# A retention and channel-mix kernel: the pieces behind the head in another order, block 3's values scaled on VectorE

## The chip, the core and the metric

The kernel runs on one core of a Trainium2 chip. The metric is the device time of one execution in microseconds (us); lower is better. Before the change the runs gave 153.27, 153.72 and 153.78 us, median 153.72.

## What is computed

There are 4 sequences of 768 tokens and 8 heads of 64 channels. The first half is a recurrence over tokens in which a 64x64 state of each head decays by its own factor; the second half is a channel mix on 512 channels with 1024 hidden ones.

```
state = gamma * state + outer(k[t], v[t])          # per sequence and head
x[t]  = scale * q[t] @ state                       # heads side by side: 512 channels
xk = mu_k * x + (1 - mu_k) * x_prev                # x_prev: the token before
xr = mu_r * x + (1 - mu_r) * x_prev
out = sigmoid(xr @ w_r) * (relu(xk @ w_k)**2 @ w_v)
```

## The kernel before

**Tiling.** The tokens are cut into 12 blocks of 256, three for each sequence; block n belongs to sequence n // 3. A block is computed in closed form: masked scores within it, and a state carried from the block before. The channel mix then runs on the block's output, which is kept transposed (channels in partitions, tokens along the line) in float32.

**An order written by hand.** The program is a list of short words, the string ORDER (lines 24 to 81). Line 755 goes through the words and calls one small function for each, so the order of the words is the order of instructions on every engine. A word is a code, its block and further indices, then `~v`, `~a`, `~p` or `~s` for the engine (VectorE, ScalarE, GpSimd, SyncE) and `@` with the numbers of the PSUM banks that a product writes. The framework adds the semaphores: each instruction waits for what it reads, and for readers of what it overwrites. Engines otherwise run freely, each through its own list.

The words that matter, with n the block:
- `lk`, `lq`, `lv` load keys, queries and values (line 222; keys and queries are cast to float16 on the way, so they go by GpSimd's queue); `wk`, `wr`, `wv` load the weights of the mix. The buffers are rings of 4, so `lq.11` waits until `Tq.7` has read block 7's queries.
- `vs` scales the values by powers of gamma (line 253), into a ring of 3.
- `Tq`, `Tk` transpose queries and keys on TensorE; `Eq`, `Ek` copy them out of PSUM on ScalarE (line 241).
- `S` makes scores (lines 318, 331), `M` masks them on VectorE (lines 347, 354). `C` makes the state's products from keys and scaled values (lines 366, 384), `U` adds them to the carried state (line 419), `G` decays it for the next block (line 424 on ScalarE, line 428 on VectorE).
- `I`, `Y`, `J` make the block's output: from the carried state, from the masked scores, and from the state again (lines 441, 462, 478). `D` scales it into xT (lines 507, 514), `dx` takes differences of neighbouring tokens (line 529), `X.n.0` and `X.n.1` mix four slices each for xk and xr (line 558); for block 0 `t` and another form of `X` do it (lines 542, 552).
- `K` are the first channel products (lines 572, 582), `Qa` takes the relu out of PSUM and `Qb` squares it, both on ScalarE (lines 591, 599, 603). `R` is the gate's product (line 612), `s` its sigmoid on ScalarE (line 618). `V` are the value products (line 624), `O` multiplies value and gate on VectorE (line 630), `st` stores (line 637). `Vc`, `Oc`, `sc` are V, O, st on half the columns, for the last piece.
- `z` are products of zeros on TensorE in the head.

Blocks 3 and 4, 6 and 7, and 9 and 10 are mixed as pairs: one product of 512 columns instead of two of 256. TensorE's pieces have two kinds of form: K, R, V and Vc use the array whole (128x128), T, S, C, I, Y and J use halves or quarters of it (128x64, 64x128, 64x64), several at a time.

Any two pieces in one PSUM bank follow one another: the second starts when ScalarE or VectorE has read out the first. There are eight banks.

The first 82 words are the head; K.0.0, the first channel product, follows just behind.

Of the kernel before, what the change touches and what calls it, by code (L numbers as in the profile page):

```python
# [43 lines left out]
O.1.0~v Tq.6@23 Eq.6~a Tk.6@01 Ek.6~a st.0.0~s lk.7~p st.1.0~s V.1.1.0@5 V.1.1.1 O.1.1~v s.2.0~a
R.2.1@2 s.2.1~a lv.5~p X.3.0.0~v X.3.0.3~v Tk.7@67 Ek.7~a G.4~a S.6@01 M.6~v Tk.5@45 Ek.5~a vs.5~v
V.2.0.0@2 K.3.2@3 Qa.3.2~a K.3.0@6 S.5.0@45 M.5.0~v S.5.1@01 C.5@3 U.5.0~v K.3.3@7 Qb.3.2~a Qa.3.0~a
lq.7~p K.3.7@6 Qa.3.3~a Qa.3.7~a lv.6~p lq.8~p vs.6~v M.5.1~v V.2.0.1 st.0.1~s I.5@67 O.2.0~v
st.2.0~s C.6@45 U.6.0~a U.6.1~v U.6.2~v K.3.6@3 Qa.3.6~a lk.9~p X.3.1.3~v Y.5 Tq.7@01 Eq.7~a U.6.3~v
# [1 line left out]
Qb.3.7~a Qa.3.1~a Qb.3.1~a dx.5~v K.3.4@0 K.3.5@1 Qa.3.5~a X.5.0.0~v X.5.0.3~v R.3.1@4 s.3.1~a  # L50
lv.7~p Qa.3.4~a X.5.0.1~v Qb.3.4~a R.3.0@1 R.4.0@4 s.3.0~a s.4.0~a Qb.3.0~a X.5.0.2~v vs.7~v K.5.2@0
S.7@67 st.1.1~s M.7~v Qb.3.5~a Y.6 Qb.3.6~a lv.10~p C.7@45 U.7.0~v X.5.1.1~v Qa.5.2~a K.5.0@1
R.4.1@6 Qa.5.0~a D.6~v s.4.1~a V.4.0.0@0 V.4.0.1 V.3.1.0@1 U.7.1~v Qb.5.0~a X.5.1.3~v U.7.2~v I.7@23
X.5.1.2~v U.7.3~v Tq.8@67 Eq.8~a X.5.1.0~v O.4.0~v lv.8~p vs.8~v Qb.5.2~a lq.10~p lk.8~p Tk.8@45
Ek.8~a V.3.1.1 V.3.0.0@0 C.8@67 O.3.1~v st.2.1~s st.3.1~s Y.7 dx.6~v D.7~v Tq.10@45 V.3.0.1 Eq.10~a
G.7~a dx.7~v X.6.0.2~v V.4.1.0@1 R.5.1@4 s.5.1~a K.5.3@2 Qa.5.3~a R.5.0@4 U.8.0~v O.3.0~v V.4.1.1
lv.9~p lk.10~p lq.9~p Tk.10@23 s.5.0~a U.8.1~v X.6.0.1~v Ek.10~a X.6.0.0~v Tk.9@45 Ek.9~a K.5.1@7
Qa.5.1~a X.6.0.3~v K.6.0@0 lq.11~p Qb.5.1~a Qa.6.0~a U.8.2~v I.8@23 vs.9~v S.8@45 M.8~v O.4.1~v
st.4.1~s K.6.4@7 Qa.6.4~a vs.10~v X.6.1.2~v K.6.2@6 C.9@45 Qa.6.2~a Qb.6.2~a U.9.0~a Y.8 U.9.1~v
D.8~v U.9.2~v U.9.3~v X.6.1.3~v Qb.5.3~a Tq.9@01 V.5.1.0@6 V.5.1.1 O.5.1~v Eq.9~a lk.11~p K.6.3@7  # L60
Qa.6.3~a K.6.7@0 Qa.6.7~a V.5.0.0@7 C.10@01 Qb.6.0~a X.6.1.0~v S.9@45 M.9~v G.9~a Qb.6.3~a Tq.11@23
Eq.11~a V.5.0.1 dx.8~v X.6.1.1~v st.4.0~s K.6.1@6 Qb.6.7~a Qa.6.1~a Qb.6.1~a X.8.0.3~v X.8.0.0~v
U.10.0~v U.10.1~v K.6.5@2 Qa.6.5~a st.3.0~s lv.11~s K.6.6@6 Qa.6.6~a Qb.6.6~a R.6.0@3 s.6.0~a
O.5.0~v U.10.2~v U.10.3~v R.7.0@6 s.7.0~a R.6.1@7 s.6.1~a I.9@01 X.8.0.2~v S.10@23 Tk.11@45 Ek.11~a
X.8.0.1~v K.8.1@7 Qb.6.5~a Qa.8.1~a Qb.8.1~a vs.11~v st.5.1~s K.8.0@6 C.11@45 M.10~v Qb.6.4~a
X.8.1.0~v X.8.1.2~v Y.9 D.9~v G.10~a U.11.0~v st.5.0~s U.11.1~v U.11.2~v Qa.8.0~a I.10@23 V.6.1.0@7
V.6.1.1 O.6.1~v V.6.0.0@0 V.6.0.1 I.11@45 S.11@67 M.11~v dx.9~v V.7.1.0@1 V.7.1.1 Y.10 D.10~v
dx.10~v X.9.0.3~v X.9.0.0~v Y.11 Qb.8.0~a X.9.0.2~v R.7.1@6 s.7.1~a X.9.0.1~v V.7.0.0@7 V.7.0.1
K.8.3@6 O.7.0~v X.9.1.0~v D.11~v X.8.1.1~v Qa.8.3~a Qb.8.3~a K.8.2@2 Qa.8.2~a Qb.8.2~a X.8.1.3~v
dx.11~v X.11.1.0~v X.11.1.1~v X.9.1.1~v V.8.1.0@6 K.9.2@3 X.11.0.0~v K.9.6@7 Qa.9.6~a V.8.1.1  # L70
Qa.9.2~a Qb.9.2~a X.11.0.3~v K.9.5@7 K.9.3@3 K.9.0@2 Qa.9.0~a Qb.9.6~a V.8.0.0@4 V.8.0.1 Qb.9.0~a
Qa.9.5~a Qb.9.5~a Qa.9.3~a O.7.1~v st.7.1~s X.9.1.2~v X.11.0.1~v O.6.0~v K.9.7@5 R.8.1@7 s.8.1~a
# [727 lines left out]
```

## Time and profile before

| | before |
|---|---|
| median of the runs | 153.72 us |
| the profiled execution, its own time | 153.78 us |
| its span, first to last instruction | 152.0 us |
| start of K.0.0 | 18.99 us |
| end of TensorE's last product | 148.85 us |
| TensorE, VectorE, ScalarE, GpSimd busy | 144.9, 127.9, 103.8, 55.3 us |
| granted clock of TensorE | 1.00 |

The span leaves out 1.78 us of the execution's own time around it. Engines work at the same time, so their busy times don't add up. A matmul's end is modelled, and one may look busy while it waits for its operands; how far products stand apart tells more than how long each lasts. The chain that ended last is followed from the last instruction back to what released it, and each row gives a start, a length and the line.

### The profile page before, as it was taken

What the parts mean: (1) busy time and instruction counts of PE and PEld (TensorE: products, weight loads), DVE (VectorE), ACT (ScalarE), POOL (GpSimd) and SP (SyncE); (2) the same over time, 40 slices, a digit from 0 to 9 for tenths busy, and PEclk for the clock granted to TensorE, in tenths of its full rate; (3) what the DMA queues carried; (4) which work ended last, traced back from release to release, by engine and by line L of the source; (5) the groups of instructions that cost most, each with busy time, mean ns of one, the idle gap of its engine ahead of it and who ended that gap; (6) DMA issues with size and microseconds to landing.
All of it is one profiled execution on the core that took longest, in us unless ns stands there. A gap on an engine that the chain in (4) does not pass through costs nothing.

```text
span 152.0 us, 5541 instructions
## 1 busy us (share of the span) xinstructions
PE 144.9 (95%) x2426; PEld 83.2 (55%) x2426; DVE 127.9 (84%) x212; ACT 103.8 (68%) x195; POOL 55.3 (36%) x65
## 2 busy tenths in 40 slices
...
GB/s 134 220 229 196 208 227 195 169 245 211 197 166 206 222 261 113 240 314 201 231 173 125 4 46 278 101 45 35 0 4 0 4 0 202 212 0 0 147 134 138
DMA packets 45624, 22.16 MB, mean 146 GB/s; under 512 B 37400, under 2 KB 41248, under 8 KB 45600
## 3 DMA queue, kind: packets, MB, share of 16 engines
...
q8 instruction: 19, 0.31, 0.9%
...
## 4 chain that ended last, share of the span: by engine, by line
PE 73%; DMA 12%; POOL 11%; issue 1%; DVE 0%; POOLq 0%
PE ps L624 27%; PE ps L572 14%; DMA v<-in_v_dram 12%; PE ps L612 12%; PE ps L582 8%; PE ps L278 3%; POOL q L235 3%; POOL k L230 2%; PE ps L441 2%; POOL vs L253 2%; POOL v L230 2%; PE ps L366 1%; PE ps L462 1%; PE ps L642 1%; PE ps L318 1%
## 5 line engine op out<-in xcount | busy, mean ns | idle before, releaser
L624 PE MATMUL ps<-wv,k2s 128*128 128x512 f16 x184 | 44.1, 380 | 0.0
L591 ACT ACTIVATE kr<-ps 128x512 f32<-128x512 f32 x48 | 27.9, 594 | 13.0 <-PE ps L582 7.1
L624 PEld LDWEIGHTS <-k2s 128*128 128x128 f16 x184 | 17.1, 98 | 18.9 <-ACT k2s L603 0.4
L630 DVE SCALAR_TENSOR_TENSOR os<-ps,rs 128x512 f32<-128x512 f32 x23 | 15.6, 684 | 11.9 <-ACT rs L618 9.4
L612 PE MATMUL ps<-wr,xr 128*128 128x512 f16 x96 | 23.5, 379 | 0.0
L572 PE MATMUL ps<-xk,wk 128*128 128x512 f16 x96 | 23.3, 379 | 0.0
L582 PE MATMUL ps<-xk,wk 128*128 128x256 f16 x192 | 23.2, 273 | 0.0
L618 ACT ACTIVATE rs<-ps 128x512 f32<-128x512 f32 x24 | 13.7, 597 | 13.0 <-PE ps L612 12.4
L230 POOL DMA_DIRECT2D k<-in_k_dram x20 | 17.8, 902 | 10.9 <-PE ps L384 6.8
L582 PEld LDWEIGHTS <-wk 128*128 128x128 f16 x192 | 18.1, 98 | 3.7
L558 DVE SCALAR_TENSOR_TENSOR xr<-dx,mu,xT 128x256 f16<-128x256 f32 (+1 forms) x32 | 17.9, 577 | 0.1
L241 ACT COPY qT<-ps 128x1024 f16<-128x1024 f16 (+1 forms) x13 | 12.3, 946 | 8.2 <-PE ps L278 7.8
L230 POOL DMA_DIRECT2D v<-in_v_dram x18 | 16.0, 912 | 3.7 <-DVE a L354 1.9
L558 DVE SCALAR_TENSOR_TENSOR xk<-dx,mu,xT 128x256 f16<-128x256 f32 (+1 forms) x32 | 17.0, 579 | 0.2
L572 PEld LDWEIGHTS <-wk 128*128 128x128 f16 x96 | 9.1, 98 | 10.8 <-issue 0.5
L603 ACT ACTIVATE k2s<-kr 128x512 f16<-128x512 f32 x24 | 14.8, 631 | 0.3
L612 PEld LDWEIGHTS <-xr 128*128 128x128 f16 x96 | 9.0, 98 | 10.7 <-issue 0.5
L354 DVE TENSOR_TENSOR a<-ps,c_sb 128x1024 f16<-128x1024 f32 (+1 forms) x14 | 14.6, 1065 | 0.2 <-PE ps L331 0.2
L599 ACT ACTIVATE k2s<-kr 128x512 f16<-128x512 f32 x24 | 14.5, 627 | 0.3
L241 ACT COPY kT<-ps 128x1024 f16<-128x1024 f16 (+1 forms) x13 | 12.2, 946 | 2.8 <-PE ps L272 2.0
L529 DVE TENSOR_TENSOR dx<-xT 128x1024 f32<-128x1024 f32 x11 | 13.4, 1222 | 0.2
L253 DVE TENSOR_TENSOR vs<-v,csm_sb 128x1024 f16<-128x1024 f32 x10 | 12.2, 1216 | 0.4 <-DMA v<-in_v_dram 0.4
...
## 6 DMA issues: line engine op xcount, KB each, us to landing
out_dram<-os SPq DMA_DIRECT2D x23, 256.0 KB, 2.5
v<-in_v_dram POOLq DMA_DIRECT2D x18, 256.0 KB, 7.7
q<-in_q_dram POOLq DMA_DIRECT2D x11, 256.0 KB, 8.1
...
```

The source lines that it names most:

```text
L230: e.dma_start(out=dst[:, :, i * D : i * D + D], in_=src[:, i * P : i * P + P].rearrange("h p d -> p h d"),)
L241: e.copy(out=out, in_=in_)
L253: e.tensor_tensor(out=VS(n), in0=V32(n).rearrange("p h (i d) -> p i h d", i=2), in1=gks[:, int(half(n) or wide(n)), :, :, None].to_broadca ...
L354: nc.vector.tensor_tensor(out=a_full(n)[:, i, :, j0:j1], in0=pairs(banks("S", n, i, j0))[:, :, j0:j1], in1=(below if wide(n) else causal[: ...
L558: nc.vector.scalar_tensor_tensor(out=XM[w](k)[:, j, t0:t1], in0=DX(k)[:, j, t0:t1], scalar=mu[:, w * NCO + j : w * NCO + j + 1], in1=x[:, ...
L572: nc.tensor.matmul(banks("K", n, g), lhsT=wk16[:, co, g * P : g * P + P], rhs=XM[0](k)[:, co, :], start=(co == 0), stop=(co == NCO - 1),)
L582: nc.tensor.matmul(pz[:, i, :], lhsT=wk16[:, co, fo * P : fo * P + P], rhs=XM[0](k)[:, co, m * TM + t0 : m * TM + t1], start=(i == 0 and c ...
L591: nc.scalar.activation(out=kr, in_=banks("K", n, g, *u), func=AF.Relu)
L603: nc.scalar.activation(out=K2(n)[:, w * g : w * g + w, t0:t1], in_=kr.rearrange("p a t -> p (a t)").rearrange("p (i t) -> p i t", i=w), fu ...
L612: nc.tensor.matmul(banks("R", n, tb), lhsT=XM[1](k)[:, co, t : t + P], rhs=wr16[:, co, :], start=(co == 0), stop=(co == NCO - 1),)
L624: nc.tensor.matmul(banks("V", n, tb), lhsT=K2(n)[:, fo, tb * P : tb * P + P], rhs=wv16[:, fo, :], start=(fo == 0), stop=(fo == NFO - 1),)
L630: nc.vector.scalar_tensor_tensor(out=OS(2 * n + tb), in0=banks("V", n, tb), scalar=1.0 / (KSC * KSC), in1=RS(2 * n + tb), op0=ALU.mult, op ...
```

## The change

From K.0.0 on the words stand in another order, and so do the instructions on every engine; many products write other PSUM banks. The head is the same, and the words are the same 638, but for two that go to another engine: `vs.3` runs on VectorE instead of GpSimd, and `G.6` on VectorE instead of ScalarE (one multiplication of 128x256 instead of four scalings of 128x64). No function is changed. The GpSimd queue now issues lk.3, wr, lq.4, lk.4, lv.3, lq.3, lv.4 where it issued lq.4, wr, lk.4, lq.3, lk.3, lv.3, lv.4. The diff, cut to the parts that are spoken of:

```diff
-X.0.0.3~v Ek.2~a K.0.0@2 K.0.1@6 lq.4~p U.1.1~v G.1~a wr~p lk.4~p D.1~v dx.1~v X.1.0.2~v X.1.0.0~v
-K.0.2@3 Qa.0.0~a Qb.0.0~a Qa.0.2~a lq.3~p X.1.0.1~v X.1.0.3~v X.1.1.0~v Qa.0.1~a K.0.3@2 Qa.0.3~a
-lk.3~p vs.2~v Tq.2@3 X.1.1.2~v K.1.3@6 K.1.0@2 C.2@7 U.2.0~v lv.3~p Eq.2~a S.2.1@45 M.2.1~v S.2.0@01
-M.2.0~v Qb.0.3~a lv.4~p K.1.1@3 X.1.1.1~v Qa.1.0~a t.0.1.0~a K.1.2@7 I.2@45 Qb.0.1~a Qa.1.1~a wv.0~p
-Qb.0.2~a Tq.4@23 Eq.4~a Y.2 Qa.1.3~a Qb.1.1~a X.0.1.3~v X.1.1.3~v R.1.1@0 Tk.4@23 Ek.4~a J.2 R.1.0@6
-Qa.1.2~a s.1.0~a X.0.1.2~v X.0.1.1~v X.0.1.0~v R.0.1@1 s.0.1~a s.1.1~a R.0.0@7 s.0.0~a S.4.1@23
-Qb.1.0~a D.2~v dx.2~v X.2.0.2~v X.2.0.0~v S.4.0@45 Tq.3@0 Eq.3~a X.2.0.1~v wv.1~p X.2.0.3~v Tk.3@7
-lq.5~p Ek.3~a K.2.2@1 Qa.2.2~a K.2.3@0 M.4.1~v M.4.0~v Qa.2.3~a Qb.2.3~a lk.6~p S.3.1@67 M.3.1~v
-S.3.0@23 vs.3~p C.3@45 U.3.0~a Qb.2.2~a K.2.1@0 Qa.2.1~a K.2.0@4 Qa.2.0~a I.3@01 lq.6~p vs.4~v
-C.4@67 U.3.1~v X.2.1.1~v V.0.1.0@5 M.3.0~v V.1.0.0@4 G.3~a U.4.0~v I.4@23 X.2.1.3~v U.4.1~v J.3
-Qb.1.3~a Y.4 Qb.2.0~a lk.5~p X.2.1.2~v X.2.1.0~v Y.3 D.3~v dx.3~v V.0.0.0@7 V.0.1.1 O.0.1~v Tq.5@01
-J.4 D.4~v dx.4~v R.2.0@6 Qb.2.1~a V.0.0.1 O.0.0~v X.3.0.1~v Eq.5~a Qb.1.2~a V.1.0.1 X.3.0.2~v
...
-X.3.1.2~v I.6@23 J.5 X.3.1.0~v D.5~v X.3.1.1~v Qb.3.3~a G.6~a V.2.1.0@4 K.3.1@5 V.2.1.1 O.2.1~v
...
-Qa.11.2~a X.11.1.2~v O.8.0~v st.7.0~s st.8.1~s st.8.0~s V.9.1.0@5 V.10.1.0@6 s.10.0~a V.9.1.1
-V.10.0.1 s.9.1~a O.9.1~v st.9.1~s Qb.11.2~a Qb.11.3~a O.10.0~v st.10.0~s R.10.1@0 V.9.0.1 s.10.1~a
-O.9.0~v R.11.1@0 V.10.1.1 Qb.11.1~a V.11.0.0@7 R.11.0@1 s.11.0~a st.9.0~s Vc.11.1.1@5 s.11.1~a
-O.10.1~v st.10.1~s Oc.11.1.1~v V.11.0.1 O.11.0~v st.11.0~s sc.11.1.1~a Vc.11.1.0@0 Oc.11.1.0~v
-sc.11.1.0~s
+X.0.0.3~v Ek.2~a K.0.0@2 Qa.0.0~a U.1.1~v G.1~a D.1~v X.0.1.3~v dx.1~v K.0.2@3 K.0.3@2 Qa.0.3~a
+X.1.0.2~v K.0.1@4 X.1.0.0~v X.1.0.1~v Tq.2@2 Eq.2~a X.1.0.3~v vs.2~v K.1.1@5 S.2.1@67 Qa.0.2~a
+S.2.0@01 Qa.1.1~a Qb.1.1~a C.2@3 K.1.0@2 X.1.1.0~v lk.3~p Tk.3@5 M.2.1~v U.2.0~v I.2@67 wr~p
+Qb.0.0~a M.2.0~v t.0.1.0~a lq.4~p Qa.1.0~a Ek.3~a X.1.1.2~v X.1.1.1~v lk.4~p K.1.3@3 Qa.1.3~a
+Qb.1.3~a X.1.1.3~v Y.2 Qb.0.3~a X.0.1.0~v R.1.1@5 X.0.1.1~v Qa.0.1~a lv.3~p Tq.4@23 Eq.4~a J.2
+X.0.1.2~v R.0.0@0 s.0.0~a R.0.1@4 Tk.4@23 Qb.1.0~a R.1.0@0 lq.3~p Ek.4~a s.0.1~a D.2~v s.1.1~a
+Qb.0.2~a K.1.2@1 Qa.1.2~a dx.2~v X.2.0.3~v S.4.1@23 Qb.0.1~a X.2.0.1~v s.1.0~a S.4.0@67 lv.4~p
+X.2.0.0~v X.2.0.2~v vs.3~v K.2.2@5 K.2.3@4 Tq.3@0 Qa.2.3~a Eq.3~a M.4.0~v M.4.1~v C.3@67 U.3.0~a
+K.2.1@4 vs.4~v Qa.2.2~a S.3.0@01 M.3.0~v U.3.1~v S.3.1@23 M.3.1~v wv.0~p Qa.2.1~a Qb.2.1~a K.2.0@6
+Qa.2.0~a I.3@45 G.3~a C.4@01 X.2.1.2~v V.1.1.0@7 V.1.0.0@6 U.4.0~v I.4@23 U.4.1~v X.2.1.0~v wv.1~p
+lk.6~p X.2.1.1~v J.3 Y.4 X.2.1.3~v Y.3 lk.5~p D.3~v G.4~a dx.3~v V.0.0.0@1 V.0.0.1 Tk.6@45 O.0.0~v
+st.0.0~s J.4 D.4~v Qb.1.2~a lq.6~p V.1.1.1 O.1.1~v dx.4~v V.0.1.0@0 V.0.1.1 V.1.0.1 O.0.1~v Qb.2.2~a
+Qb.2.0~a Ek.6~a V.2.0.0@7 Qb.2.3~a lq.5~p Tq.5@23 Eq.5~a lv.5~p X.3.0.0~v Tk.5@01 st.0.1~s Ek.5~a
+Tq.6@45 Eq.6~a X.3.0.1~v X.3.0.2~v V.2.0.1 R.2.1@2 s.2.1~a X.3.0.3~v K.3.6@0 Qa.3.6~a O.1.0~v vs.5~v
+X.3.1.3~v R.2.0@6 X.3.1.2~v lk.7~p s.2.0~a C.5@0 S.6@23 M.6~v Tk.7@45 U.5.0~v Ek.7~a K.3.0@6 O.2.0~v
+Qa.3.0~a K.3.5@1 Qa.3.5~a X.3.1.0~v X.3.1.1~v K.3.7@6 S.5.1@01 Qa.3.7~a Qb.3.5~a S.5.0@23 lv.6~p
+lq.7~p I.5@45 K.3.2@6 Qb.3.6~a Qa.3.2~a K.3.3@7 M.5.1~v st.1.0~s V.2.1.0@6 V.2.1.1 M.5.0~v Y.5
+vs.6~v lv.7~p st.1.1~s vs.7~v lv.11~s Qa.3.3~a Qb.3.3~a O.2.1~v C.6@23 U.6.0~a U.6.1~v U.6.2~v
+st.2.1~s Tq.7@01 Qb.3.0~a Qb.3.2~a Eq.7~a J.5 D.5~v U.6.3~v dx.5~v X.5.0.3~v st.2.0~s K.3.4@7
+Qa.3.4~a R.4.1@6 s.4.1~a K.3.1@2 G.6~v Qa.3.1~a Qb.3.4~a I.6@45 X.5.0.2~v C.7@01 U.7.0~v R.3.1@3
+Qb.3.1~a s.3.1~a U.7.1~v U.7.2~v R.4.0@2 R.3.0@6 s.3.0~a U.7.3~v X.5.1.2~v V.3.1.0@3 s.4.0~a
+X.5.1.3~v I.7@67 S.7@01 M.7~v lq.11~p V.3.0.0@2 Qb.3.7~a V.3.0.1 lv.9~p lq.10~p X.5.1.0~v X.5.0.1~v
...
+lk.9~p Tk.9@45 Ek.9~a O.4.1~v st.3.1~s V.4.0.0@1 V.4.0.1 R.5.0@2 s.5.0~a O.4.0~v X.6.0.2~v st.4.0~s
+V.5.1.0@3 lq.8~p Tq.8@01 X.6.0.3~v C.8@45 lk.10~p U.8.0~v Eq.8~a C.9@67 K.6.4@2 Qa.6.4~a X.6.1.2~v
...
+vs.11~v vs.10~v I.9@67 S.9@01 M.9~v st.4.1~s Qa.6.7~a V.7.0.0@2 Qb.6.7~a Qb.6.6~a X.8.1.1~v V.7.0.1
+C.10@01 O.7.0~v Eq.11~a G.9~a U.10.0~v U.10.1~v V.6.0.0@4 st.7.0~s V.6.0.1 O.6.0~v U.10.2~v Qa.8.0~a
...
+V.9.0.1 s.9.0~a R.9.1@7 s.9.1~a Qa.11.0~a O.9.1~v st.9.1~s Qb.11.0~a R.11.0@5 Qb.11.3~a Qb.11.1~a
+R.10.1@7 V.10.0.0@1 V.10.0.1 O.9.0~v O.8.1~v K.11.2@0 V.10.1.0@6 s.10.1~a V.10.1.1 st.8.0~s st.9.0~s
+st.8.1~s O.10.1~v O.10.0~v st.10.0~s st.10.1~s V.11.0.0@2 Qa.11.2~a Qb.11.2~a V.11.0.1 s.11.1~a
+s.11.0~a O.11.0~v st.11.0~s Vc.11.1.1@1 Oc.11.1.1~v Vc.11.1.0@6 Oc.11.1.0~v sc.11.1.0~s sc.11.1.1~a
```

More of the change, by code (lines that the diff above doesn't have):

```diff
@@ L43 @@
-J.4 D.4~v dx.4~v R.2.0@6 Qb.2.1~a V.0.0.1 O.0.0~v X.3.0.1~v Eq.5~a Qb.1.2~a V.1.0.1 X.3.0.2~v
[L44 to L48, printed above, removed]
@@ L49 @@
-X.3.1.2~v I.6@23 J.5 X.3.1.0~v D.5~v X.3.1.1~v Qb.3.3~a G.6~a V.2.1.0@4 K.3.1@5 V.2.1.1 O.2.1~v
[L50 to L72, printed above, removed]
@@ L73 @@
-K.9.1@1 R.8.0@7 X.9.1.3~v X.11.0.2~v st.6.1~s O.8.1~v R.9.1@0 R.9.0@6 K.11.0@3 K.11.3@2 s.8.0~a
-Qa.9.1~a Qb.9.1~a Qb.9.3~a V.10.0.0@1 V.9.0.0@7 Qa.11.0~a Qb.11.0~a Qa.11.3~a s.9.0~a K.9.4@6
-R.10.0@2 Qa.9.7~a X.11.1.3~v st.6.0~s K.11.1@5 Qa.11.1~a Qa.9.4~a K.11.2@3 Qb.9.7~a Qb.9.4~a
-Qa.11.2~a X.11.1.2~v O.8.0~v st.7.0~s st.8.1~s st.8.0~s V.9.1.0@5 V.10.1.0@6 s.10.0~a V.9.1.1
-V.10.0.1 s.9.1~a O.9.1~v st.9.1~s Qb.11.2~a Qb.11.3~a O.10.0~v st.10.0~s R.10.1@0 V.9.0.1 s.10.1~a
-O.9.0~v R.11.1@0 V.10.1.1 Qb.11.1~a V.11.0.0@7 R.11.0@1 s.11.0~a st.9.0~s Vc.11.1.1@5 s.11.1~a
@@ new lines @@
+X.5.0.0~v Y.6 Y.7 D.6~v D.7~v dx.6~v K.5.2@0 Qa.5.2~a K.5.0@1 K.5.1@0 Qa.5.0~a Qa.5.1~a lk.8~p
+K.5.3@1 G.7~a Qa.5.3~a dx.7~v V.3.1.1 V.4.1.0@0 lv.8~p O.3.1~v X.5.1.1~v Qb.5.3~a O.3.0~v X.6.0.0~v
+vs.8~v V.4.1.1 R.5.1@1 s.5.1~a Qb.5.1~a Tq.10@23 Eq.10~a vs.9~v X.6.0.1~v Qb.5.0~a Tk.8@67 Ek.8~a
+lk.9~p Tk.9@45 Ek.9~a O.4.1~v st.3.1~s V.4.0.0@1 V.4.0.1 R.5.0@2 s.5.0~a O.4.0~v X.6.0.2~v st.4.0~s
+V.5.1.0@3 lq.8~p Tq.8@01 X.6.0.3~v C.8@45 lk.10~p U.8.0~v Eq.8~a C.9@67 K.6.4@2 Qa.6.4~a X.6.1.2~v
+U.9.0~a U.8.1~v K.6.0@0 Qa.6.0~a K.6.2@2 Qa.6.2~a X.6.1.0~v Qb.6.0~a V.5.0.0@5 K.6.3@2 Qa.6.3~a
@@ new lines @@
+Qb.6.3~a U.9.1~v Qb.5.2~a U.9.2~v U.9.3~v U.8.2~v I.8@67 S.8@01 Qb.6.2~a K.6.1@4 M.8~v X.6.1.1~v
+Qa.6.1~a K.6.6@2 Qa.6.6~a X.6.1.3~v Tk.10@01 Ek.10~a Qb.6.4~a Y.8 Qb.6.1~a D.8~v lq.9~p dx.8~v
+st.3.0~s X.8.0.3~v R.6.1@4 s.6.1~a K.6.5@2 V.5.0.1 Qa.6.5~a Qb.6.5~a X.8.1.3~v V.5.1.1 O.5.1~v
+st.5.1~s R.7.1@4 s.7.1~a lv.10~p S.10@67 X.8.1.2~v Tq.9@23 Eq.9~a lk.11~p Tk.11@01 Ek.11~a X.8.0.2~v
+O.5.0~v st.5.0~s R.6.0@4 X.8.0.0~v s.6.0~a R.7.0@5 s.7.0~a K.6.7@2 M.10~v X.8.0.1~v K.8.0@3 Tq.11@45
+vs.11~v vs.10~v I.9@67 S.9@01 M.9~v st.4.1~s Qa.6.7~a V.7.0.0@2 Qb.6.7~a Qb.6.6~a X.8.1.1~v V.7.0.1
```

9 lines of the change are left out of this document (added).

## Prediction

> **What bounds the kernel now.** I read the page's busy shares first, then the windows for the five stretches behind the head, the waits of TensorE, and the chain that ended last.
>
> ```profile
> span 152.0 us, 5541 instructions
> ...
> PE 144.9 (95%) x2426; PEld 83.2 (55%) x2426; DVE 127.9 (84%) x212; ACT 103.8 (68%) x195; POOL 55.3 (36%) x65
> ```
> ```profile
> 19.00:45.00 26.00, 24.87 (x410) 18.04 (x405) 24.56 (x39) 21.87 (x42) 19.50 (x22) 1.00 1.59 202
> 45.00:67.00 22.00, 22.00 (x411) 11.03 (x409) 21.67 (x29) 15.35 (x29) 14.41 (x17) 1.00 1.35 224
> 67.00:104.00 37.00, 37.00 (x842) 20.73 (x841) 36.27 (x59) 29.62 (x54) 7.14 (x9) 1.00 0.89 136
> 104.00:128.00 24.00, 24.00 (x343) 12.97 (x341) 22.34 (x35) 13.34 (x26) 0.00 (x0) 1.00 0.05 19
> 128.00:152.00 24.00, 20.83 (x120) 11.54 (x118) 7.14 (x13) 11.74 (x22) 0.00 (x0) 1.00 0.31 115
> ```
> ```profile
> PE ps L384 <- DVE vs L253: 0.5, 1, 0.5
> PE ps L478 <- DVE a L354: 0.4, 1, 0.4
> PE ps L384 <- POOL vs L253: 0.3, 1, 0.3
> ```
>
> In a window row the stretch's length is followed by the busy times of TensorE (24.87 in the first), its weight loads, VectorE (24.56), ScalarE and GpSimd, then clock, DMA share and GB/s. The changed part starts with K.0.0 at 18.99 us. From there TensorE idles 26.00 - 24.87 = 1.13 us up to 45 and then never until its last product. VectorE is nearly as full: 24.56 of 26.00, 21.67 of 22.00, 36.27 of 37.00. So TensorE bounds, VectorE stands just behind it, and a new order of the same pieces can win only the 1.13 us, a little that hides inside busy rows, and the tail. The clock column is 1.00 throughout and needs no further thought.
>
> **The tail** keeps its form: two half-width value products (Vc), a scaling each, a store each. Both orders end so, hence 0.
>
> ```profile
> 52.66 0.37 PE ps L278 x32
> 53.04 0.27 PE ps L318 x32
> 53.30 0.29 PE ps L278 x32
> 53.60 0.97 PE ps L624 x4
> 54.56 1.73 PE ps L572 x8
> ...
> 66.85 2.73 PE ps L612 x12
> ...
> 97.26 2.88 PE ps L572 x12
> 100.14 2.59 PE ps L612 x12
> ...
> 121.03 2.59 PE ps L572 x12
> ...
> 127.94 2.71 PE ps L612 x12
> ...
> 148.85 0.02 issue
> 148.87 0.42 DVE os L649
> ```
>
> **Changes of array shape (+0.74 us).** K, R, V and Vc use the whole 128x128 array; the transposes, scores, states and outputs (T, S, C, I, J, Y) use halves or quarters of it. The chain shows what a run of small pieces between whole ones costs beyond its own streaming. Eight whole-array products take 1.73, so four take 0.865; the four just behind small ones take 0.97, 0.10 more. The 32 transposes at 52.66, just behind whole ones, take 0.37; the same form at 53.30, behind other small ones, 0.29, 0.08 less. Together 0.185 for each run. I counted runs in both orders from K.0.0 on: 25 before, 29 after. 4 x 0.185 = 0.74. Bounds: 0, if every added run stands beside a wait that is there anyway, and 0.74.
>
> The Trainium skill, "TensorEngine Tiling (Array Packing)", Key Properties, speaks against this change too: a change of the tiling mode, not merely of the tile, drains TensorE. By that rule the changes from one small shape to another count as well, 65 after and 58 before; at some 0.1 us each that would be +0.7 us. The 0.10 and 0.08 of the chain agree with it.
>
> **Waits that go (-1.68 us).** First the 1.13 us above: C.2 waited for the scaled values of block 2 (0.5), Y.2 for masked scores (0.4), C.3 for GpSimd's scaling of block 3 (0.3). Then waits inside busy rows: twelve whole products stream in 2.59 (100.14, 121.03), but took 2.88, 2.73 and 2.71 in other places, 0.29 + 0.14 + 0.12 = 0.55 us. These are pieces that found their PSUM bank not yet read out. Order decides both kinds, so I strike them and price the new order afresh.
>
> **Waits that come, up to 45 us (+0.89 us).** I went through the new order piece by piece with the durations below.
>
> ```profile
> 18.99 3.67 PE L582 MATMUL ps<-xk,wk 128*128 128x256 f16 x32
> 22.59 0.64 PE L272 MATMUL ps<-c_sb,q 128*64 128x128 f16 x16
> 23.16 1.95 PE L582 MATMUL ps<-xk,wk 128*128 128x256 f16 x16
> 25.59 0.32 PE L384 MATMUL ps<-vs,k 128*64 128x64 f16 x8 [0.48 <-DVE vs L253]
> 25.84 0.62 PE L331 MATMUL ps<-qT,kT 64*128 64x128 f16 x16
> ```
> ```profile
> 20.54 1.23 DVE L529 TENSOR_TENSOR dx<-xT 128x1024 f32<-128x1024 f32 x1
> 21.80 1.68 DVE L558 SCALAR_TENSOR_TENSOR xk<-dx,mu,xT 128x256 f16<-128x256 f32 x4
> 23.39 0.48 DVE L558 SCALAR_TENSOR_TENSOR xr<-dx,mu,xT 128x256 f16<-128x256 f32 x1
> 24.31 1.23 DVE L253 TENSOR_TENSOR vs<-v,csm_sb 128x1024 f16<-128x1024 f32 x1 [0.43 <-DMA v<-in_v_dram]
> ```
>
> - K.1.1, +0.32. TensorE does the four K of block 0 and Tq.2 as before and reaches block 1 at 23.16. VectorE now does X.0.1.3 ahead of dx.1 (about 0.3 more), so the last of the four mixes ends at 23.48 + 0.29 = 23.77. The fourth product of K.1.1 needs it and would start at 23.16 + 0.33 = 23.49; with 0.05 for the release it starts at 23.81.
> - C.2, +0.52. vs.2 cannot start before its values land (24.31 with its wait above; the load is issued in the unchanged head), so C.2 stays at 25.59. Before it the new order puts S.2.1 and S.2.0 (two of the x16 row, 0.55 together) where the old one had K.1.0; K.1.1 leaves at 24.45, the scores have ended at 25.07.
> - I.2, Y.2, R.1.1, R.0.0, K.2.2, Tq.3, S.3.0 and I.4 come out on time by 0.0 to 0.5 us, Tq.3 by 0.05 and S.3.0 by 0.1 behind ScalarE. C.4 waits 0.05 for the masked scores of block 3.
>
> **vs.3 on VectorE, G.6 on VectorE.**
>
> ```profile
> 25.49 10.70 DMA v<-in_v_dram
> 36.19 0.07 issue
> 36.27 1.91 POOL vs L253
> ```
> ```profile
> L253 DVE TENSOR_TENSOR vs<-v,csm_sb 128x1024 f16<-128x1024 f32 x10 | 12.2, 1216 | 0.4 <-DMA v<-in_v_dram 0.4
> L424 ACT ACTIVATE tg<-t,csm_sb 128x64 f16<-128x64 f32 x32 | 8.5, 337 | 0.9 <-DVE t L419 0.9
> L419 DVE TENSOR_TENSOR tg<-ps,tg 128x256 f16<-128x256 f32 x20 | 8.4, 418 | 1.4 <-PE ps L331 0.5 <-PE ps L395 0.5 <-ACT tg L424 0.3
> ```
>
> GpSimd loses 1.9 us and ScalarE four scalings of 337 ns; VectorE gains 1.22 for vs.3 and, by its nearest row (L419), 0.42 for G.6: 1.64 us on an engine that has 1.44 us free up to 45 and 0.33 us between 45 and 67. Behind vs.3 on VectorE stand M.4.0 (frees C.3's bank), M.4.1, vs.4 and M.3.0 (frees C.4's). It is paid from the lead that VectorE has where TensorE does value products (the V pieces need nothing of it), so I book nothing for it alone; where the lead is used up is the next part. One condition: VectorE reaches vs.3 at about 34.95 (from vs.2's end at 25.54: two masks, D.2 and dx.2 at 1.2 each less their overlap, one U, eleven mixes at 0.4), and in this trace the values of block 3 landed at 36.19. In the new order lk.3 and wr go ahead, lv.3 before lq.3. One q load is 256 KB, at the 202 GB/s of the first window 1.3 us, so lv.3 should land near 34.9. This is an estimate, and it just fits.
>
> ```profile
> L230 POOL DMA_DIRECT2D v<-in_v_dram x18 | 16.0, 912 | 3.7 <-DVE a L354 1.9 <-DVE os L630 0.8 <-DMA q<-in_q_dram 0.6
> ...
> q<-in_q_dram POOLq DMA_DIRECT2D x11, 256.0 KB, 8.1
> ```
>
> On the GpSimd queue the new order holds everything behind lq.11 until Tq.7 (about 64 us) has read that buffer; the loads behind it are first needed past 80 us, and 16 issues of some 0.9 us end before. Behind lv.11 on SyncE stand stores whose buffers are needed 15 us later. Both cost 0.
>
> **Waits that come behind 45 us (+0.55 us).** VectorE has several appointments without slack: C.5 needs vs.5 and comes level with it, K.3.6 the mix X.3.0.3, I.6 the sum U.6.3, C.10 the mask M.9 (0.2 to spare). Between M.5.0 and U.6.3 VectorE has vs.6, vs.7, O.2.1, two U, D.5 and U.6.3, about 5.1 us; TensorE has 5.0 us of pieces there, so I.6 waits 0.1. Banks written again after a single whole-array piece (1.73 us for product, read-out and release) number 14, before 12; K.3.2 on bank 6 comes 0.07 early. The old order paid 0.55 of hidden waits, I take the same 0.55 for the new one, the 0.1 and 0.07 in it. Bounds: 0, and 14 x 0.15 = 2.1 if each pays what the dearest hidden ones paid (0.29 for two).
>
> **Sum.** +0.74 - 1.68 + 0.89 + 0.55 = +0.50 us on the profiled execution's 153.78 (span 152.0 and 1.78 around it): **154.3 us**. The median of the runs is 153.72, 0.06 lower, so this is slower by 0.4%.
>
> **Rivals.**
> 1. The values of block 3 land late (0.16). If the order of loads doesn't help and they land at 36.19 again, VectorE stands 1.2 us at vs.3, and as C.4 has no slack all of it reaches TensorE: 155.5; half of it, 154.9. For it: the 10.70 us from issue to landing. Against: a q load less ahead.
> 2. Banks bind (0.12): six or seven of the 14 reuses pay 0.15, another 1.0 us: 155.3. For: ScalarE has Qb or a copy queued ahead of several read-outs. Against: most of the old 12 paid nothing.
> 3. Not slower: the added runs of small pieces stand beside waits (0.32). A drain costs nothing where the next piece waits anyway. S.2.0 to C.2, C.3, I.6 are such places. If it covers all four runs, -0.74: 153.5; with late waits at half as well, 153.2. It decides when each wait named above exceeds 0.1 us and lies at a change of shape.
>
> That nothing changes at all is excluded: each engine's order differs from K.0.0 on.
>
> **How the numbers follow.** Forecast 0.40, centred at 154.3 (153.9 to 154.7); rivals 0.16, 0.12 and 0.32. A measurement of this kernel tells 0.3% (0.46 us) from no change, so "same" is 153.26 to 154.18. Rival 3 lies half below that and half in it (0.16 each); of the forecast 0.14 lies in it and 0.26 above; rivals 1 and 2 lie above. Faster 0.16, same 0.30, slower 0.54. The range runs from 153.1 (rival 3 almost whole) to 155.5 (rival 1 whole); about 0.06 stays out on each side.
>
> **What would show it.** Right: TensorE's idle time from K.0.0 on is about 0.6 us (C.2, little else), its last product ends near 149.3, VectorE's vs.3 starts near 35.0 with no wait for DMA, and twelve-product rows above 2.59 recur. Wrong: a wait of TensorE over 0.5 us that isn't C.2's (then a step above was missed), vs.3 waiting for its load (rival 1), or a busy time of TensorE no larger than 128.71 - 0.55 over the same five stretches (rival 3).

## The result and the profile after

The changed kernel takes 156.19 us (156.02 to 156.36, 4 runs), the kernel before beside it 153.75 (153.27 to 153.93, 4 runs): 1.0164 times as long, 95% interval 1.0138 to 1.0189. The forecast was 154.3, its range ended at 155.5. The sign was right, the size was not: 2.4 us were lost where 0.5 were expected. The profiled execution took 156.25 us, 1.75 of it outside its span. Line numbers of after are one lower than before's, those of the experiments three.

The page of after, its busy shares, and from the queues the one that carries TensorE's program:

```profile
span 154.5 us, 5543 instructions
...
PE 146.5 (95%) x2426; PEld 83.5 (54%) x2426; DVE 129.5 (84%) x214; ACT 102.5 (66%) x191; POOL 53.4 (35%) x64
...
q8 instruction: 19, 0.31, 0.8%
```

Its windows, by the stretches that were used for before (the last ends with the span):

```profile
19.00:45.00 26.00, 25.76 (x443) 18.00 (x435) 25.65 (x41) 21.65 (x45) 19.43 (x24) 1.00 1.64 203
45.00:67.00 22.00, 21.10 (x395) 10.69 (x394) 21.18 (x27) 14.16 (x23) 4.52 (x6) 1.00 0.80 158
67.00:104.00 37.00, 37.00 (x748) 20.21 (x746) 34.42 (x56) 27.53 (x49) 15.34 (x18) 1.00 1.08 163
104.00:128.00 24.00, 24.00 (x446) 13.48 (x445) 22.17 (x34) 11.93 (x26) 0.00 (x0) 1.00 0.17 61
128.00:154.60 26.60, 22.48 (x128) 12.23 (x125) 10.54 (x20) 15.36 (x29) 0.00 (x0) 0.98 0.22 79
```

Up to 45 us TensorE idles 0.24 us, before it was 1.13: the waits that were to go went. But there is 22.00 - 21.10 = 0.90 between 45 and 67, where before had none, and in the last stretch, whose last product ends at 151.36 us, 23.36 - 22.48 = 0.88. TensorE's waits name the two, as two of its rows:

```profile
PE ps L277 <- issue: 0.9, 1, 0.9
PE ps L641 <- DVE os L629: 0.9, 1, 0.9
```

**The first stop** lies inside one piece, Tq.6, the transposes of block 6's queries. TensorE's timeline around it:

```profile
51.22 0.44 PE L277 MATMUL ps<-c_sb,q 64*64 64x64 f16 x32
51.50 0.44 PE L277 MATMUL ps<-c_sb,k 64*64 64x64 f16 x32
51.76 0.33 PE L277 MATMUL ps<-c_sb,q 64*64 64x64 f16 x15
52.98 0.32 PE L277 MATMUL ps<-c_sb,q 64*64 64x64 f16 x17 [0.90 <-issue]
53.24 1.04 PE L623 MATMUL ps<-wv,k2s 128*128 128x512 f16 x4
```

Fifteen of 32 transposes run, then nothing for a microsecond, then the other 17. They are one piece, and no semaphore stands between them; "issue" says that the profile shows nothing that TensorE waited for. Tq.6 takes 53.24 - 51.76 = 1.48 us until the next piece, where the same piece elsewhere takes 0.40 (e8_loads, below): 1.08 us lost.

What ran out was the program. The window from 0 to 52.95 us counts what TensorE had begun by then:

```profile
0.00:52.95 52.95, 49.02 (x861) 30.32 (x862) 49.09 (x90) 37.51 (x74) 37.51 (x46) 1.00 1.50 208
```

That is 861 products and 862 weight loads, and the trace has six sequencer instructions of TensorE besides: 1729, or 6 x 256 + 193. The instruction queue of the page above brought 19 packets of 16 KB for TensorE's 4862 instructions, 256 in each. The packet before this place is seen in the DMA view: none from 46 to 50.3 us (first row, where only the data's queue stands), one from 50.3 to 51.5.

```profile
q0 software_dynamic: 2494, 0.97, 164.5%
```
```profile
q0 software_dynamic: 497, 0.29, 141.7%
q8 instruction: 1, 0.02, 5.3%
```

By its record it started at 50.41 and had landed at 51.43; the next instruction ran at 52.98. In before the packet of the same place started at 49.23, landed at 50.50, and TensorE reached the border at 52.69, too late to notice. In after TensorE had entered the block ahead of the border at 46.40: 4.0 us to the packet's start, 1.0 to its landing and 1.6 to the next instruction make 6.6, and TensorE was through that block in 5.5.

**The second stop** is in the tail. VectorE's timeline from 140 us, then the chain that ended last:

```profile
141.46 1.89 DVE L629 SCALAR_TENSOR_TENSOR os<-ps,rs 128x512 f32<-128x512 f32 x3 [7.50 <-ACT rs L617]
148.11 1.89 DVE L629 SCALAR_TENSOR_TENSOR os<-ps,rs 128x512 f32<-128x512 f32 x3 [4.77 <-DMA out_dram<-os]
```
```profile
143.58 4.41 DMA out_dram<-os
...
148.72 0.69 DVE os L629
149.41 0.04 issue
149.45 1.92 PE ps L641 x16
```

The first three are O.9.1, O.9.0 and O.8.1, the next O.10.1, O.10.0, O.11.0. The output buffers are four; O.10.1 takes that of O.8.1. In before O.8.1 was done at 129.6 us, over 10 us ahead of O.9.1 and O.9.0:

```profile
128.88 0.69 DVE L630 SCALAR_TENSOR_TENSOR os<-ps,rs 128x512 f32<-128x512 f32 x1
```

In the new order it stands behind O.9.1 and O.9.0, its store is the last of four on SyncE, leaves at 143.58 and takes 4.41 us (the three ahead of it took 2.03, 2.35 and 3.13, in before the store of O.8.1 took 2.01). O.10.1 waits for it, and O.10.0 behind it on VectorE is what frees bank 1 for the last but one product. TensorE has sixteen products of V from 144.95 and would start that Vc 3.45 us later, as it does in e1_tail; it starts 4.50 us later: 1.05 lost.

**The balance.** K.0.0 started at 19.52 in this execution against 18.99 (the head is the same); C.2 cannot start before vs.2 ends, at 25.54 in both profiles, so the later head was made good there:

```profile
25.64 0.32 PE L383 MATMUL ps<-vs,k 128*64 128x64 f16 x8
```

From C.2 to the end of the last product are 151.36 - 25.64 = 125.72 us, before 148.85 - 25.59 = 123.26: +2.46. Less 1.08 and 1.05 there remain +0.33, where the forecast had +0.50.

### The profile page after: what moved, and what is told of

It is laid out like the page before. It is cut to its first block, busy times and chain, and to the rows that moved or that the text cites. A ratio compares the mean times of both kernels' runs of the same rounds, so it can differ in the third digit from the quotient of the medians.

```text
span 154.5 us, 5543 instructions
## 1 busy us (share of the span) xinstructions
PE 146.5 (95%) x2426; PEld 83.5 (54%) x2426; DVE 129.5 (84%) x214; ACT 102.5 (66%) x191; POOL 53.4 (35%) x64
## 4 chain that ended last, share of the span: by engine, by line
PE 81%; DVE 8%; issue 3%; DMA 3%; ACT 3%; SPq 0%; DVEq 0%; ACTq 0%
PE ps L623 23%; PE ps L571 14%; PE ps L611 13%; PE ps L581 10%; PE ps L702 4%; PE ps L277 4%; DMA out_dram<-os 3%; PE ps L440 2%; DVE a L353 2%; DVE os L629 2%; PE ps L271 2%; PE ps L477 1%; PE ps L641 1%; PE ps L461 1%; PE ps L317 1%
## 5 line engine op out<-in xcount | busy, mean ns | idle before, releaser
L623 PE MATMUL ps<-wv,k2s 128*128 128x512 f16 x184 | 43.6, 379 | 0.0
L581 PE MATMUL ps<-xk,wk 128*128 128x256 f16 x192 | 24.0, 273 | 0.1
L571 PE MATMUL ps<-xk,wk 128*128 128x512 f16 x96 | 22.6, 379 | 0.0
L557 DVE SCALAR_TENSOR_TENSOR xr<-dx,mu,xT 128x256 f16<-128x256 f32 (+1 forms) x32 | 17.4, 577 | 0.0
L234 POOL DMA_DIRECT2D q<-in_q_dram x12 | 10.7, 899 | 16.8 <-PE ps L440 16.3
```

The costliest lines, as they stand in the source:

```text
L557: nc.vector.scalar_tensor_tensor(out=XM[w](k)[:, j, t0:t1], in0=DX(k)[:, j, t0:t1], scalar=mu[:, w * NCO + j : w * NCO + j + 1], in1=x[:, ...
L571: nc.tensor.matmul(banks("K", n, g), lhsT=wk16[:, co, g * P : g * P + P], rhs=XM[0](k)[:, co, :], start=(co == 0), stop=(co == NCO - 1),)
L581: nc.tensor.matmul(pz[:, i, :], lhsT=wk16[:, co, fo * P : fo * P + P], rhs=XM[0](k)[:, co, m * TM + t0 : m * TM + t1], start=(i == 0 and c ...
L623: nc.tensor.matmul(banks("V", n, tb), lhsT=K2(n)[:, fo, tb * P : tb * P + P], rhs=wv16[:, fo, :], start=(fo == 0), stop=(fo == NFO - 1),)
```

## The experiments

Theory: the forecast's sum holds, and two things that it priced at nothing cost about 1.1 us each: a block of TensorE's program that lands late, and a store buffer. Rivals: VectorE, by then with vs.3 and G.6 on it, holds TensorE back in places that the trace doesn't name; or the changes of array shape cost more than was booked.

### The two stops, one at a time

**e1_tail**, on after:

```diff
-K.11.0@2 X.11.1.1~v R.11.1@3
+K.11.0@2 X.11.1.1~v O.8.1~v st.8.0~s st.8.1~s R.11.1@3
-O.9.0~v O.8.1~v K.11.2@0 V.10.1.0@6 s.10.1~a V.10.1.1 st.8.0~s st.9.0~s st.8.1~s
+O.9.0~v K.11.2@0 V.10.1.0@6 s.10.1~a V.10.1.1 st.9.0~s
```

> The changed kernel, with O.8.1 moved forward on VectorE to just behind X.11.1.1 (it stood behind O.9.0), and st.8.0 and st.8.1 moved ahead of st.9.1 on SyncE; nothing else. Theory (store buffer): in the changed kernel O.10.1 waits 4.8 us for st.8.1 to land because O.8.1 came 8 us later than it could, the buffer ring has four places, O.10.0 stands behind O.10.1 on VectorE, and the last half-width product needs O.10.0's bank: 0.9 us of TensorE. Then VectorE's 4.8 us wait for a store is gone, TensorE has no wait ahead of the half-width products, and the time falls by 0.9 to 1.1 us, to 155.1 to 155.3. Rival (the end is set by the value products and ScalarE, the store only happens to land then): the wait moves to another releaser and the time stays within 0.3 us of 156.2.

Measured: 155.05 us (154.37 to 156.02, 10 runs), ratio to before 1.0076 [1.0042, 1.011]. VectorE's second group no longer waits for a DMA, and the last products start 3.45 us after the sixteen:

```profile
146.25 1.29 DVE L627 SCALAR_TENSOR_TENSOR os<-ps,rs 128x512 f32<-128x512 f32 x2 [4.19 <-ACT rs L615]
```
```profile
144.27 3.62 PE L621 MATMUL ps<-wv,k2s 128*128 128x512 f16 x16
147.72 1.91 PE L639 MATMUL ps<-wv,k2s 128*128 128x256 f16 x16
```

The second stop is settled: 1.1 us, and it is the store buffer.

This edit leaves TensorE's list and the loads around the first stop as they are in after, so its profile shows that stop a second time:

```profile
51.81 0.33 PE L275 MATMUL ps<-c_sb,q 64*64 64x64 f16 x15
52.31 0.32 PE L275 MATMUL ps<-c_sb,q 64*64 64x64 f16 x17 [0.17 <-issue]
52.56 1.04 PE L621 MATMUL ps<-wv,k2s 128*128 128x512 f16 x4
```

The pause is at the same instruction, but Tq.6 takes 0.75 us and not 1.48: the packet started at 49.55 here, at 50.41 in after's profile. The 1.08 us is the price in one execution, and this one paid 0.35.

**e2_burst**, on after: Tq.6 and its copy stand behind V.2.0.1, so that only 64 transposes come in one run.

```diff
-Tk.5@01 st.0.1~s Ek.5~a Tq.6@45 Eq.6~a X.3.0.1~v X.3.0.2~v V.2.0.1 R.2.1@2
+Tk.5@01 st.0.1~s Ek.5~a X.3.0.1~v X.3.0.2~v V.2.0.1 Tq.6@45 Eq.6~a R.2.1@2
```

> The changed kernel, with Tq.6 (32 small transposes) moved behind V.2.0.1 (four whole products) instead of ahead of it, so that Tq.5, Tk.5 and Tq.6 no longer stand in one run of 96 small products; nothing else. Theory (code loading): the pause of 1.1 us in the middle of Tq.6 is TensorE out of instructions; its 1729th instruction (6 x 256 + 193) had not been loaded. Then the pause is gone or below 0.2 us, one more change of array shape costs 0.2, and the time falls by 0.7 to 1.0 us, to 155.2 to 155.5. Rival (something that Tq.6 itself needs is late: its bank, its queries): Tq.6 waits less only by the 0.96 us of products put ahead of it, TensorE's last product ends where it did, and the time stays within 0.3 us of 156.2 or the pause stays inside Tq.6 with the time unchanged.

Measured: 155.68 us (155.54 to 156.00, 4 runs), 1.0106 [1.0045, 1.0166]. The pause is gone from Tq.6. The gain of 0.5 is below the 0.7 to 1.0 expected, and the interval overlaps that of after: the edit adds a run of small pieces (0.19, below), and in this execution the tail's wait was 1.2 us.

**e3_shift64** and **e4_shift192**, on after: Tq.4 is issued twice, or four times (the repeats write the same values), so that everything behind it stands 64 or 192 instructions further on.

```diff
-Tq.4@23 Eq.4~a
+Tq.4@23 Tq.4@23 Eq.4~a
```

> The changed kernel with Tq.4 issued twice (32 transposes more, that is 64 instructions of TensorE, same result), some 20 us ahead of the pause. Theory (code loading): instruction 1729 is now one that stood 64 earlier in the program, so the pause moves out of Tq.6 into Tk.5, about half way through it (16 of 32 transposes done). Rival (a need of Tq.6): the pause stays in Tq.6 behind its 15th transpose. Time by either: 0.2 to 0.4 us above the changed kernel for the 32 transposes.

> The changed kernel with Tq.4 issued four times (96 transposes more, 192 instructions). Theory (code loading): instruction 1729 now lies ahead of the run of small transposes, among whole products that take 108 ns an instruction, and the next block begins behind the run, so no pause over 0.3 us is left between 50 and 56 us; the 96 transposes cost 0.8 us where TensorE has nothing to hide them, so the time is 155.7 to 156.2, at or below the changed kernel's 156.2. Rival (a need of Tq.6): the pause stays in Tq.6 and the time is 156.7 to 157.2.

Measured: e3 157.77 us (2 runs), 1.0238 [1.0142, 1.0335]; e4 161.06 and 164.18 us, no ratio (the granted clock in its profile was 0.979, 0.93 between 20 and 40 us, so the places of its pauses count and not their lengths). Both expected times missed, and in e3 the expected place too. The waits of e3, and the worst pause of e4:

```profile
PE ps L579 <- issue: 2.0, 2, 1.6
PE ps L275 <- issue: 1.2, 1, 1.2
```
```profile
34.13 0.25 PE L275 MATMUL ps<-c_sb,k 64*64 64x64 f16 x8
38.35 0.54 PE L275 MATMUL ps<-c_sb,k 64*64 64x64 f16 x24 [3.96 <-issue]
```

The pause did leave Tq.6, as the theory had it. In e3 it didn't come up in Tk.5, at the new place of instruction 1729: the block ahead of it lasted 7.6 us there. But new ones came up where I hadn't looked: in e3 at TensorE's instructions 1217, 1985 and 2753, in e4 at 1217, 2753 and 3265. All of these are 193 beyond a multiple of 256, as 1729 is, and in no run does a pause of TensorE's products of 0.2 us or more that ends in "issue" stand anywhere else. In e3 one lies in K.5.0, whole-array products, so the form of the piece doesn't matter. In e4 the added transposes themselves ran into the border at 1217 and waited about 4 us. The cause holds; what I could not foretell was the next victim, since with every piece moved each border has a new distance to its packet.

**e8_loads**, on after: TensorE's list stays word for word as it is.

```diff
-S.5.0@23 lv.6~p lq.7~p
+S.5.0@23 lq.7~p
...
-st.1.0~s V.2.1.0@6
+st.1.0~s lv.6~s lv.7~s V.2.1.0@6
...
-vs.6~v lv.7~p st.1.1~s
+vs.6~v st.1.1~s
```

> The kernel after, but the loads of the values of blocks 6 and 7 are issued on SyncE behind st.1.0 instead of on GpSimd, so 512 KB less data is under way when TensorE's eighth code block is fetched (50.41 us). If data traffic delays the fetch, it starts at least 1 us earlier and the 1.1 us pause in Tq.6 falls under 0.3: 155.0 to 155.5. Rival: the fetch is triggered by TensorE's own progress and takes the same time whatever the traffic: the fetch stays near 50.4, the pause near 1.1, the time 156.0 to 156.4. The loads come later than before; if the values of block 6 land after 59 us, VectorE waits for them and this adds.

Measured: 155.81 us (155.57 to 156.17, 4 runs), 1.0133 [1.0116, 1.0149]. The DMA view from 48.8 to 49.9 us, and Tq.6 in TensorE's timeline:

```profile
q8 instruction: 1, 0.02, 5.5%
```
```profile
51.74 0.47 PE L275 MATMUL ps<-c_sb,q 64*64 64x64 f16 x32
52.14 1.04 PE L621 MATMUL ps<-wv,k2s 128*128 128x512 f16 x4
```

With two value loads fewer in the queues the packet starts at 48.87 instead of 50.41, and the 32 transposes run through: V.2.0.1 starts 1.10 us earlier. So the packet waits behind data, by more or less from one execution to the next: with the loads of after it started between 49.55 and 50.61 (after, e1, e2, e5), with two fewer between 48.20 and 49.81 (e8, and e9 and e12 below). Only 0.4 us arrive at the end, less than expected, and the interval overlaps that of after. In this execution the last products waited 1.19 us on the store buffer, 0.14 more than in after; and other executions of after may have paid less than 1.08, as e1's did, which their times don't tell.

### Both together

**e5_both** is e1 and e2 on after; **e9_tail_loads** is e1 and e8 on after, with TensorE's list untouched.

> The kernel after with both edits: O.8.1 behind X.11.1.1 on VectorE with st.8.0 and st.8.1 ahead of st.9.1 on SyncE, and Tq.6 with its copy behind V.2.0.1. If the two losses are the store buffer in the tail (about 1.05 us) and the code block inside Tq.6 (0.5 by its own run, 1.1 by the pause), they add: 156.19 - 1.1 - 0.5 to 1.1 = 154.0 to 154.6, and what is left against 153.75 is the forecast's own remainder, +0.3 to +0.9. Rival: the two overlap, or the block's pause only moves to another border, and it stays at 155.0 or above.

> The kernel after with both losses removed and every instruction of TensorE in its place: the tail as in e1_tail, the loads of the values of blocks 6 and 7 on SyncE as in e8_loads. If the two losses are all that the prediction left out, 156.19 - 1.05 - 1.1 = 154.05, and its own sum (154.3) is what remains: 153.9 to 154.6. Rival: something else of 0.5 us or more is hidden in the new order, and it stays above 154.9.

Measured: e5 154.37 us (153.87 to 155.25, 10 runs), 1.0044 [1.0026, 1.0063]; e9 154.62 (154.29 to 155.73, 12 runs), 1.0052 [1.0025, 1.0079]. By the ratios that is +0.68 us (0.40 to 0.97) and +0.80 (0.38 to 1.2) on the runs of before beside them, forecast +0.5; in e5's the run of small pieces that it adds is about 0.19. The rest of the sum holds within what can be measured. Taking the pause away is worth 0.4 to 0.7 us by the medians (e8 and e2 against after, e9 and e5 against e1), with intervals that overlap each time: less than the 1.08 of after's profile. The last product of e5 ends at 147.71 + 1.91 = 149.62 us, forecast near 149.3:

```profile
147.71 1.91 PE L639 MATMUL ps<-wv,k2s 128*128 128x256 f16 x16
```

### The price of a run of small pieces

**e10_split**, on BEFORE: four runs of small pieces are cut by a whole-array product next to them. One of the four:

```diff
-Tk.8@45 Ek.8~a V.3.1.1 V.3.0.0@0
+V.3.1.1 Tk.8@45 Ek.8~a V.3.0.0@0
```

> The kernel BEFORE, with four runs of small pieces each cut in two by a whole-array product that stands beside it: Tk.6 behind V.1.1.0, Tk.8 behind V.3.1.1, Tk.9 behind K.5.1 and V.7.1.0 ahead of S.11; all other engines keep their order. The prediction prices a run at 0.185 us: 4 x 0.185 = +0.74, 154.4 to 154.6. Rival: the change of shape is hidden, or its price is not paid per run: 153.6 to 153.9, no difference from before.

Measured: 155.55 us (155.29 to 155.73, 4 runs), 1.0112 [1.0097, 1.0128]: +1.72, more than either expected. The place of Tk.8, before and e10, from Tq.8 (76.04, 76.28) to C.8 (78.52, 78.96):

```profile
76.04 0.44 PE L278 MATMUL ps<-c_sb,q 64*64 64x64 f16 x32
76.30 0.45 PE L278 MATMUL ps<-c_sb,k 64*64 64x64 f16 x32
76.69 1.90 PE L624 MATMUL ps<-wv,k2s 128*128 128x512 f16 x8
78.52 0.38 PE L366 MATMUL ps<-vs,k 64*64 64x64 f16 x20
```
```profile
76.28 0.44 PE L275 MATMUL ps<-c_sb,q 64*64 64x64 f16 x32
76.65 1.04 PE L621 MATMUL ps<-wv,k2s 128*128 128x512 f16 x4
77.62 0.45 PE L275 MATMUL ps<-c_sb,k 64*64 64x64 f16 x32
78.00 1.04 PE L621 MATMUL ps<-wv,k2s 128*128 128x512 f16 x4
78.96 0.38 PE L363 MATMUL ps<-vs,k 64*64 64x64 f16 x20
...
120.40 1.67 PE L569 MATMUL ps<-xk,wk 128*128 128x512 f16 x7 [0.64 <-DVE xk L555]
```

2.48 us became 2.68: 0.20 for the added run. The other three places show 0.21, 0.19 and 0.19. So the price of 0.185 is right, and 0.79 of the 1.72 is it. The largest other piece, 0.80, is the last row: S.11 starts 1.22 us after I.11 where it was 0.15, since V.7.1.0 now stands between them; its mask and the mixes behind it on VectorE came late, and K.9.2 waited behind its first product. Delaying a small piece by one product had a second price that neither theory had.

### vs.3 and G.6

**e6_pool3** is e5 with vs.3 on GpSimd again, at the same place; **e11_vs3dve** is BEFORE with vs.3 on VectorE, between M.4.1 and M.4.0; **e12_g6act** is e9 with G.6 on ScalarE.

```diff
-vs.3~v
+vs.3~p
```

> The same as e5_both, but the values of block 3 are scaled on GpSimd again, at the same place of the order. If VectorE's 1.22 us for them lies under value products, as the prediction booked it: within 0.3 us of e5_both, or up to 0.5 slower, since GpSimd needs 1.91 us from the same start and C.3 then waits about 0.3 to 0.7 us more. Rival: VectorE is the bound there, and without it the time falls by 0.5 to 1.2 us below e5_both.

> The kernel BEFORE, with one edit: the values of block 3 are scaled on VectorE, between the masks M.4.1 and M.4.0. As the prediction has it (1.22 us lie under value products, nothing is paid): 153.5 to 153.9. Rival: in the old order GpSimd ran beside masks, which it doesn't slow (three in 3.55 us), so the move only loads VectorE, the scaled values of block 4 come 1.2 us later and C.4 waits for them some 0.5 to 1.0 us: 154.2 to 154.8.

> The same as e9_tail_loads, but G.6 is on ScalarE again (four scalings of 128x64 in place of one multiplication on VectorE). The prediction booked nothing for it: within 0.3 us of e9_tail_loads. Rival: VectorE's 0.42 us are paid in full, and it is 0.3 to 0.5 us faster without them.

Measured: e6 155.94 us (155.72 to 156.28, 4 runs), 1.0142 [1.0123, 1.0161], 1.57 us SLOWER than e5 beside it, a result that neither theory had. e11 154.55 (154.28 to 155.44, 12 runs), 1.0034 [1.0004, 1.0065]. e12 155.23 (154.50 to 155.84, 12 runs), 1.0077 [1.0052, 1.0102].

In e6 three timelines tell it: GpSimd's, one mix of VectorE's (from 35 us on), and TensorE's K.2.2.

```profile
34.38 2.18 POOL L250 TENSOR_TENSOR vs<-v,csm_sb 128x1024 f16<-128x1024 f32 x1 [4.58 <-DMA v<-in_v_dram]
```
```profile
34.71 2.12 DVE L555 SCALAR_TENSOR_TENSOR xk<-dx,mu,xT 128x256 f16<-128x256 f32 x1
```
```profile
36.89 0.39 PE L579 MATMUL ps<-xk,wk 128*128 128x256 f16 x2 [0.95 <-DVE xk L555]
```

The mix X.2.0.0, third of four, takes 2.12 us where each of the others takes 0.48: it ends 0.28 after GpSimd's scaling, which ends at 36.56. This mix stands still until GpSimd is through, and K.2.2 waits 0.95. In before GpSimd's scaling ran beside masks, and those three took 3.55 us together; two with no GpSimd beside them take 2.35 in after, as much for each. The Trainium skill, "SBUF — State Buffer", section "SBUF: two separate sides", says that VectorE and GpSimd share a port pair as an exclusive lock, and that a VectorE operation with two SBUF inputs is fully blocked while a GpSimd operation that reads SBUF holds it; the mixes read two tensors there, the masks one and PSUM, and the 2.12 against 0.48 agrees. About 1.0 of the 1.57 us is this place; in e6's profile another 0.38 comes from a wait for the first weights in the unchanged head, the rest is not placed.

In the old order vs.3 on VectorE costs about 0.5 us (e11): M.4.0 comes later, and C.3 writes a bank that M.4.0 has yet to read (C.3's row among the waits of e11):

```profile
PE ps L381 <- DVE a L351: 1.1, 1, 1.1
```

In e12 R.4.0 starts 0.4 us later against e9: its bank is read out late by ScalarE, which now has four scalings more ahead of that.

```profile
PE ps L609 <- ACT kr L588: 0.2, 1, 0.2
```

So G.6 on VectorE cost nothing, as booked, and spared about 0.4; the medians differ by 0.6, but their intervals overlap. The rival that VectorE, with these two on it, holds TensorE back is out: without either the kernel was no faster.

### A place of the new order in the old

**e14_c2late**, on BEFORE, to have the gain of one wait that went:

```diff
-C.2@7 U.2.0~v lv.3~p Eq.2~a S.2.1@45 M.2.1~v S.2.0@01 M.2.0~v
+lv.3~p Eq.2~a S.2.1@45 M.2.1~v S.2.0@01 C.2@7 M.2.0~v U.2.0~v
```

> The kernel BEFORE, with one place of the new order in it: C.2 stands behind S.2.1 and S.2.0 on TensorE, and U.2.0 behind the two masks on VectorE. The wait of C.2 (0.48) then lies under the scores and the masks start some 0.5 us earlier, so that Y.2's wait (0.36) shrinks too: 0.4 to 0.8 us gained, 152.9 to 153.3. Rival: the wait moves to the next product that needs VectorE (R.1.1, then K.2.2), and the time stays within 153.6 to 153.9.

Measured: 156.40 us (155.97 to 156.57, 6 runs), 1.0146 [1.011, 1.0182], a miss by 3 us.

```profile
28.86 1.03 PE L579 MATMUL ps<-xk,wk 128*128 128x256 f16 x8 [1.33 <-DVE tg L416]
```

This is K.1.2, which takes bank 7 behind C.2; with U.2.0 behind two masks the bank comes free 1.3 us later, and K.2.2 then waits 1.1 for VectorE's mixes. That second wait is the one of e6 again, as VectorE's and GpSimd's timelines show:

```profile
34.98 3.39 DVE L555 SCALAR_TENSOR_TENSOR xk<-dx,mu,xT 128x256 f16<-128x256 f32 x4
```
```profile
35.78 1.92 POOL L250 TENSOR_TENSOR vs<-v,csm_sb 128x1024 f16<-128x1024 f32 x1
```

The four mixes take 1.67 us in before, where they end at 35.58 and GpSimd scales from 36.27 on. Here they are a microsecond later, vs.3 runs beside them, and they take 3.39. The new order has C.2 in bank 3, with U.2.0 between the masks. No version here beats the kernel before.

## Why the prediction was wrong, by its own steps

- **"The tail keeps its form ... hence 0": failed, 1.05 us.** The form of the last two products is the same, but what stands ahead of them is not. The prediction looked at products and banks there, and not at the ring of four output buffers, where O.10.1 follows O.8.1. On SyncE it asked for the stores behind lv.11 (rightly 0) and not for the last six.
- **No term for the program's own loading: failed, 1.08 us in after's profile, 0.4 to 0.7 by the medians.** The pieces between 46 and 53 us were summed as if instructions were always there. The order puts 96 small transposes in one run, 192 instructions, and a block of 256 went by in 51.9 - 46.4 = 5.5 us, before 52.7 - 46.2 = 6.5.
- **Array shapes, +0.74: held.** 0.19 to 0.21 a run in e10, against 0.185. The 65 and 58 changes that the prediction counts beside it are all changes of shape in the traces, those to and from whole pieces among them; between two small shapes there are 7 after and 8 before. So the +0.7 that it works out from them stands in place of the 0.74 and not on top of it.
- **Waits that go, -1.68: held as far as they show** (idle up to 45 us 0.24, before 1.13).
- **Waits up to 45 us, +0.89: held, with another split.** C.2 started at 25.64, expected 25.59. K.1.1 took 0.43 more than its streaming (0.32 expected) and C.2's wait was spent by the later head.
- **Behind 45 us, +0.55: not measured by itself;** with the rest it comes to +0.33 in after's profile and to +0.68 and +0.80 in the runs of e5 and e9. That the sum comes so near to +0.50 doesn't show that each of its terms is right.
- **vs.3 and G.6, 0: held for the time, not for the reason.** The condition was met: vs.3 started at 35.11 (expected 35.0) and waited for no load, so rival 1 didn't occur. But the prediction weighed 1.22 us on VectorE against 1.9 on GpSimd, and not what GpSimd does to the mixes beside it. In this order GpSimd would have cost 1.0 us or more.
- **Rivals.** 2 and 3 didn't decide: e5 and e9 leave neither another 1.0 us for banks nor -0.74 for hidden runs, and TensorE's busy time over the five stretches rose from 128.70 to 130.34 us, where rival 3 asked for no more than about 128.15. The sentence "a wait of TensorE over 0.5 us that isn't C.2's (then a step above was missed)" named what happened, twice.
